# What holds back a gather: other F tiles for the holds, an earlier place for one block's gathers, and two scalings moved in the last unit

## The chip, the core and the metric

The kernel runs on one core of a Trainium2 chip. Its engines work from queues of their own and wait for each other through semaphores: PE (TensorE, matrix products; PEld is its weight loads), DVE (VectorE), ACT (ScalarE), POOL (GpSimd), and SP, whose queue issues the large loads. The metric is the device time of one execution in microseconds. Three runs of the kernel before took 372.48, 372.81 and 375.04 us; the median is 372.81.

## The reference, cut to what matters

A recurrent attention block is followed by a mixture of eight experts, of which each token uses one. All is float32.

```python
# attention, per batch b and head h, over t: state is 48x48
y[:, :, t] = einsum('bhd,bhde->bhe', rt, state + u*kt*vt)
state      = w * state + einsum('bhd,bhe->bhde', kt, vt)
# experts, per token x[b, s] of 384 numbers
e = argmax(logits) if s == 0 or local_gate < 0.5 else prev_e     # top expert or the previous token's
p = softmax(logits)
h = maximum(x[b, s] @ w1[e], 0.0)                                # 384 -> 1024
out[b, s] = p[e] * (h @ w2[e])                                   # 1024 -> 384
```

There are 4 x 768 tokens. A token's expert is known only when its attention output and the router's choice are there; its row is then gathered from memory, and its result scattered back.

## The kernel before, in words

The first part, up to about 105 us, is attention, and is not touched. The rest is the class Experts. It works through ten units, each one expert and a number of token slots. Units 0 and 1 are **plain** units of 168 slots (`HEAD`), worked while the router still sorts the second half of the tokens. Units 2 to 9 are the **blocks** of `BLOCKS = (448, 424, 392, 376, 336, 336, 256, 192)`, the experts in falling order of their token counts. Units 2 to 7 are **wide** (336 slots or more); unit 8 has a form of its own; unit 9, the last, is plain again. Unit 2 is the first large block, unit 3 the second, unit 4 the third with 392 slots: three gathers of 128 rows and a fourth of 8.

A unit's tokens come by `gather` (L1157): one indirect DMA from POOL's queue for each 128 rows, from `x_d` into a tile `xg`. PE turns `xg` (transposes, L1170) and ACT copies the result to `exT`. Then come the hidden layer (L1184 in plain units, L1265 in wide ones), the relu, and the second product (L1281, L1322, L1332, L1425). ACT scales a result by its gate (L1410, L1460), and POOL scatters it (L1415).

The hidden layer's result lies in eight **F tiles**, `u[0]` to `u[7]`, four in each tile `hg`. In a plain unit the relu (L1187) writes u[m] as soon as PE has done step m. In a wide unit a step of `twenty(i, g, ...)` makes tiles 4g to 4g + 3 by a scheme with fewer products: in ten steps s = 0 to 9, PE adds into two banks, ACT copies them out to `snap` (L1268), DVE joins these pieces in `hg` (L1252), and ACT does the relu (L1257 and L1260) **in place** on the same columns. The relus are put off by `self.owed`: u[4g + 2] gets its relu in step 5; u[4g] and u[4g + 1] only in step 0 of the half that follows, so u[4] and u[5] of a unit get theirs in step 0 of the next unit.

All engines' orders are written out by hand: the order of the calls in the code is the order of each queue. A gather would go out as soon as POOL reaches it. To hold it back, `gather` may have a tile `after`; POOL then first copies one column of that tile to a small tile `seen` (L1153), and so waits until it is written. `gathered(i, j, after)` does this for the gather j of unit i. The copy reads the tile as it stands at that place in the order; a write that comes later in the order has to wait until the copy has read.

Two other things lie near the change. In unit 1, at m = 4, POOL writes one element of unit 2's `w2t` from the last rows gathered for unit 2 (L1506), and SP loads that `w2t` only behind this. And `xg` has six buffers, so a gather also waits until the rows that were in its buffer have been turned. `weight_sums` (L1222, DVE) and `factors` (L1300, DVE) are sums of weights that the schemes need; `sums` (L1291, DVE) are those of F tiles.

In unit 9, at m = 2, the products of unit 8 are finished; `joined` makes DVE's seven steps (L1392), and `ends` holds the two scalings (ACT, L1410), each with its scatter.

Of the kernel before, what the change touches and what calls it, by code (L numbers as in the profile page):

```python
# [27 lines left out]
DK, FK = D // P, F // P  # L28
# [9 lines left out]
EARLY = 2  # L38
# [1029 lines left out]
class Experts:  # L1068
# [447 lines left out]
    def run(self, att, flag, ready, free):  # L1516
# [39 lines left out]
        def gathered(i, j, after):  # L1556
            if i < n and j < len(self.units[i]["rows"]):
                self.gather(i, slice(j, j + 1), after)
# [5 lines left out]
        def wide(i, g, s):  # L1564
            nonlocal behind
            u, r = self.units[i], self.router
            following = self.units[i + 1]["wide"]
            k, z = (i, 0) if g else (i - 1, 1)
            early = k < EARLY
            if s == 0:  # L1570
                behind = {} if early else self.seven(k, z)
                if early:
                    behind = {("1b", "3a")[m - FK + 2]: lambda m=m: self.output(k, m) for m in range(FK - 2, FK)}
            if s in (1, 2) and not early:
                self.sums(k, 2 * z + s - 1)
            at = (g * 10 + s - (5 if i == EARLY else 1))
            if (i, g, s) == (EARLY, 0, 2):
                self.routing(2 * FK)
            if (i, g) == (EARLY + 1, 0):
                for when, step in ((1, r.exceeded), (2, lambda: self.flag(0)), (3, lambda: r.halves(0)), (5, lambda: r.halves(E - 1)),  # L1580
                                 (6, lambda: self.flag(1, self.bank("fp"))), (8, lambda: self.flag(2))):
                    if s == when:
                        step()
            if at >= 0 and at % 2 == 0 and at < 8:
                turned(i + 1, at // 2)
            elif (g, s) in ((0, 9), (1, 1), (1, 3), (1, 5), (1, 7), (1, 9)) and (i, g) > (EARLY, 0):
                sent()
            fill(*BEHIND[s])
            if g == 0:
                if s == 0 and not early:  # L1590
                    fs.extend(self.factors(k, 3))
                if s == (8 if i == EARLY else 3):
                    fs.extend(self.factors(i, 0))
                some(fs, (0, 0, 0, 0, 0, 0, 0, 0, 2, 2)[s] if i == EARLY else (2, 1, 1, 3, 1, 0, 0, 0, 0, 0)[s])
                if s == 5 and following:
                    ws.extend(self.weight_sums(i + 1))
                some(ws, (0, 0, 0, 0, 0, 0, 0, 2, 2, 2)[s] if i == EARLY else (0, 0, 0, 0, 0, 3, 4, 3, 3, 0)[s])
                if i == EARLY and s == 4:
                    drained(k)
                    self.fetch(i + 1, self.nc.sync, 2)  # L1600
                if s == 9 and not early:
                    joined(k)
                    some(js, 3)
                if s == 8:
                    gathered(i + 2, 0, u[2])
            else:
                if s == 0:
                    gathered(i + 2, 1, u[0])
                    some(js, 9)
                some(ends, (0, 0, 1, 1, 0, 0, 0, 0, 0, 0)[s])  # L1610
                if s == 2:
                    fs.extend(self.factors(i, 1))
                    if following:
                        ts.extend(self.token_sums(i + 1))
                if s == 7:
                    fs.extend(self.factors(i, 2))
                some(ws, (3, 2, 1, 0, 0, 0, 4, 0, 0, 0)[s] if i == EARLY else (0, 2, 1, 0, 0, 0, 0, 0, 0, 0)[s])
                some(fs, (0, 0, 1, 3, 0, 0, 0, 1, 2, 1)[s])
                some(ts, (0, 0, 0, 0, 2, 4, 4, 2, 0, 0)[s])
                if s == 5:  # L1620
                    gathered(i + 2, 2, u[6])
                if s == 9:
                    gathered(i + 2, 3, u[4])

        for i in range(n):
            u = self.units[i]
            after = len(self.units[i + 1]["rows"]) if i + 1 < n else 0
            following = i + 1 < n and self.units[i + 1]["wide"]
            if u["wide"]:
                if i == EARLY:  # L1630
                    free()
                    self.snap = self.spare.tile([P, 6, 2, BLOCKS[0] // 2], F32, name="snap", tag="xT")
                self.fetch(i + 1, self.nc.sync, 1)
                for g in range(2):
                    self.twenty(i, g, lambda s: wide(i, g, s))
                continue

            if u["seven"]:

                order = [k for ks in BEHIND for k in ks if k != "hr"]  # L1640
                parts = (0, 1, 4, 8, 12, 15, 18)
                for m in range(FK):
                    if m == 0:
                        self.fetch(i + 1, self.nc.sync, 1)
                        behind = self.seven(i - 1, 1)
                        fs.extend(self.factors(i - 1, 3))
                    self.hidden(i, m)
                    self.settle()
                    if m < 2:
                        self.sums(i - 1, 2 + m)  # L1650
                    some(fs, 4)
                    fill(*order[parts[min(m, 6)]:parts[min(m + 1, 6)]])
                    if m in (2, 3):
                        fs.extend(self.factors(i, m - 2))
                    if m == 5:
                        joined(i - 1)
                        some(js, 9)
                    if m > 5:
                        some(ends, 1)
                    if m in (3, 4):  # L1660
                        turned(i + 1, m - 3)
                    else:
                        sent()
                continue

            lag = 4 if i == n - 1 else 1
            for m in range(FK):
                if following and m == FK - 1:
                    turned(i + 1, after - 1)
                self.hidden(i, m)  # L1670
                if (i, m) == (0, 0):
                    att.turn(B * HP - 1, yb[1:])
                if i == n - 1:
                    if m == 0:
                        behind = {**self.seven(i - 1, 0)}
                        for j in range(2):
                            self.sums(i - 1, j)
                        fill(*order)
                        for j in range(2, 4):
                            some(self.factors(i - 1, j), 4)  # L1680
                            self.sums(i - 1, j)
                    if m == 1:
                        behind = self.seven(i - 1, 1)
                        fill(*[k for k in order if k[1] == "a"])
                    if m == 2:
                        fill(*order)
                        joined(i - 1)
                        some(js, 9)
                        some(ends, 2)
                if sends and m >= 1 and i > EARLY:  # L1690
                    self.send(*sends.pop(0))
                if i == n - 1:
                    if m >= lag:
                        self.rows(m - lag)
                elif m >= lag and not (following and m > FK - 3):
                    self.output(i, m - lag)
                if i <= EARLY:
                    self.routing(i * FK + m)
                if i == 0 and m == 1:
                    self.fetch(1, self.nc.scalar)  # L1700
                if m >= FK - after and not (following and m == FK - 1):
                    (turned if following else self.turn)(i + 1, m - (FK - after))
                if following and m == 3:
                    ws.extend(self.weight_sums(i + 1))
                if following and m >= 3:
                    some(ws, 4)
            if i + 1 == EARLY:
                for j in range(len(self.units[i + 2]["rows"])):
                    gathered(i + 2, j, u[FK - 2 + j // 2])

            if following:
                self.output(i, FK - 3)
                some(self.token_sums(i + 1), 12)
                self.both = False
            elif i < n - 1:
                for m in range(FK - lag, FK):
                    self.output(i, m)
                drained(i)
# [198 lines left out]
```

## Time and profile before

| What | us |
|---|---|
| median of three runs | 372.81 |
| the profiled execution, as timed | 373.39 |
| its span in the trace | 371.7 |
| PE busy | 356.4 |
| DVE busy | 268.9 |
| POOL busy | 171.1 |
| ACT busy | 152.3 |

The granted TensorE clock was 0.993 of full speed over the span. PE is busy nearly throughout. In a time line, a row gives the start, the busy time, the engine, the line, the operation with its output and inputs, and in brackets the idle time ahead of it with what ended that. In a list of waits, a row gives who waited for whom, then the sum, the number of times and the longest.

### The profile page before, as it was taken

The page shows a single profiled execution, that of the slowest core. Times are in us where ns is not written, and L with a number is a line of the kernel's source. Part 1 is how long each engine was busy: PE and PEld are TensorE (multiplying, and loading weights), DVE is VectorE, ACT ScalarE, POOL GpSimd, SP SyncE. Part 2 cuts the span into 40 slices and gives each one's busy share as a digit, 9 for nine tenths or more (in the row PEclk, how much of TensorE's full clock was granted, in tenths as well). Part 3 has the DMA queues.
Part 4 walks back from the last instruction along what each step waited for, and adds up shares of the span by engine and source line. Part 5 has one row for each costly group of instructions (what it writes and reads, how often), then busy time and mean ns, then how long its engine had stood idle before and what let it go on. Part 6 is the DMA issues. An engine that isn't in the chain of part 4 may idle for free. (4 is left out here: it accounts for less than half of the span.)

```text
span 371.7 us, 9208 instructions
## 1 busy us (share of the span) xinstructions
PE 356.4 (96%) x3542; PEld 309.4 (83%) x3542; DVE 268.9 (72%) x766; ACT 152.3 (41%) x375; POOL 171.1 (46%) x212
## 2 busy tenths in 40 slices
PE   7999999899999999899799999999999999999992
PEld 4777877677679999788689999998998998889971
DVE  6887778788834877597689869879989957446400
ACT  4222232223523224654446546556555545423110
POOL 8879999689522056148274214403604114002022
PEclk9999999999999999999999999999999999999997
DMA  7999999982668656814116506426236426505011
GB/s 270 410 409 407 408 401 359 379 285 96 203 212 288 261 204 266 337 46 173 53 48 240 186 11 229 140 94 227 91 143 232 136 82 233 182 21 213 2 44 38
DMA packets 17380, 74.91 MB, mean 202 GB/s; under 512 B 2394, under 2 KB 6240, under 8 KB 15024
## 3 DMA queue, kind: packets, MB, share of 16 engines
q1 hardware_dynamic: 10336, 56.89, 41.0%
q0 software_dynamic: 3424, 9.48, 7.5%
q10 hardware_dynamic: 3568, 7.87, 5.7%
q8 instruction: 30, 0.49, 0.5%
q14 instruction: 22, 0.18, 0.1%
HBM read 64.79 MB, written 9.47 MB: 200 GB/s over the span
## 5 line engine op out<-in xcount | busy, mean ns | idle before, releaser
L1268 ACT COPY snap<-h 128x336 f32<-128x336 f32 (+4 forms) x120 | 57.6, 480 | 77.3 <-PE h L1265 74.6
L1415 POOL DMA_INDIRECT out_dram<-yo,sid x27 | 33.4, 1238 | 92.8 <-ACT yo L1410 77.1
L1157 POOL DMA_INDIRECT xg<-x_d,gid x29 | 31.6, 1090 | 28.6 <-DVE gid L924 19.3
L1153 POOL COPY seen<-hg 128x1 f32<-128x1 f32 x26 | 16.5, 633 | 54.3 <-ACT hg L1257 49.5
L1252 DVE TENSOR_TENSOR hg<-snap 128x336 f32<-128x336 f32 (+4 forms) x48 | 26.6, 554 | 19.5 <-ACT snap L1268 19.3
L1265 PE MATMUL h<-xs,ws 128*128 128x168 f32 (+4 forms) x192 | 39.4, 327 | 0.0
L1322 PE MATMUL y<-factors,sums 128*128 128x192 f32 x168 | 38.4, 327 | 0.0
L1184 PE MATMUL h<-exT,w1t 128*128 128x168 f32 (+2 forms) x192 | 37.1, 332 | 0.0
L324 DVE TENSOR_TENSOR am<-pair,kept 128x768 f32<-128x768 f32 x32 | 29.9, 951 | 9.9 <-PE pair L314 5.9
L1265 PEld LDWEIGHTS h<-xs,ws 128*128 128x128 f32 x192 | 32.5, 190 | 4.6 <-issue 1.2
L238 POOL TENSOR_TENSOR pd<-rk 128x384 f32<-128x384 f32 x32 | 31.8, 1015 | 7.6 <-PE y L295 5.6
L1184 PEld LDWEIGHTS h<-exT,w1t 128*128 128x128 f32 x192 | 31.0, 190 | 2.7 <-issue 0.5
L1322 PEld LDWEIGHTS y<-factors,sums 128*128 128x128 f32 x168 | 28.5, 190 | 0.1
L1332 PE MATMUL tp<-w2t,hg 128*80 128x384 f32 (+2 forms) x64 | 24.7, 488 | 1.9 <-ACT hg L1257 1.9
L1187 ACT ACTIVATE hg<-h 128x168 f32<-128x168 f32 (+2 forms) x32 | 10.6, 333 | 38.0 <-PE h L1184 37.1
L1322 PE MATMUL y<-w2t,hg 128*128 128x192 f32 x112 | 25.0, 328 | 0.0
L255 POOL TENSOR_TENSOR rw<-rk,tab 128x384 f32<-128x384 f32 x26 | 23.6, 929 | 0.9 <-DMA rk<-in_rk_dram 0.9
L352 ACT COPY xT<-y 128x768 f32<-128x768 f32 x15 | 12.0, 800 | 28.2 <-PE y L344 28.2
L331 PE MATMUL y<-am,kv 128*64 128x128 f32 x360 | 22.9, 277 | 0.3 <-DVE y L301 0.3
L234 POOL TENSOR_TENSOR ke<-kv,endT 128x288 f32<-128x288 f32 (+1 forms) x32 | 21.9, 705 | 1.5 <-DMA kv<-in_kv_dram 1.5
L1300 DVE TENSOR_TENSOR factors<-w2t 128x192 f32<-128x192 f32 x56 | 19.7, 351 | 2.9 <-PE y L1322 2.9
L1222 DVE TENSOR_TENSOR ws<-w1t 128x256 f32<-128x256 f32 x48 | 18.8, 418 | 3.6 <-DMA w1t<-in_w_dram 3.6
(293 smaller groups left out, 785.1 us busy)
## 6 DMA issues: line engine op xcount, KB each, us to landing
w1t<-in_w_dram SPq DMA_DIRECT2D x8, 1536.0 KB, 6.8
w2t<-in_w_dram SPq DMA_DIRECT2D x8, 1536.0 KB, 7.1
rk<-in_rk_dram SPq DMA_DIRECT2D x15, 768.0 KB, 9.8
kv<-in_kv_dram SPq DMA_DIRECT2D x16, 584.0 KB, 8.7
vT<-in_vT_dram SPq DMA_DIRECT2D x16, 384.0 KB, 7.4
x_d<-x ACTq DMA_DIRECT2D x4, 1152.0 KB, 9.3
w1t<-in_w_dram SPq DMA_DIRECT2D x2, 768.0 KB, 5.2
w2t<-in_w_dram SPq DMA_DIRECT2D x2, 768.0 KB, 4.7
```

Source lines behind the costliest of these rows:

```text
L238: nc.gpsimd.tensor_mul(t["pd"][:, z], t["rT"][:, z], t["kT"][:, z])
L255: engine.tensor_mul(t["rw"][:, z], t["rT"][:, z], spread(pw, 1, z.stop - z.start))
L324: return lambda: nc.vector.tensor_mul(t["am"][:, g], sc, spread(kept, 1, 2))
L331: nc.tensor.matmul(t["y"][h][p * DP:(p + 1) * DP, c2 * P:(c2 + 1) * P], lhsT=t["v"][:, (2 * c + h) * DH:(2 * c + h) * DH + DP], rhs=t["am" ...
L1157: self.nc.gpsimd.indirect_dma_start(out=xg[:n], out_offset=None, in_=self.x_d[:rows], in_offset=bass.IndirectOffsetOnAxis(ap=u["gid"][:n, ...
L1184: nc.tensor.matmul(h[:, :n], lhsT=u["w1"][:, m, kk, :], rhs=u["xT"][:, kk, :], start=(kk == 0), stop=(kk == DK - 1))
L1252: return lambda: nc.vector.tensor_tensor(o, a, self.snap[:, b, :, :n], op=Alu.add if op == "+" else Alu.subtract)
L1265: nc.tensor.matmul(bank[:, z * n:(z + 1) * n], lhsT=left(a), rhs=right(b), start=(k == 0 and z == 0), stop=(k == len(CHAINS[c]) - 1), skip ...
L1268: nc.scalar.copy(self.snap[:, place, :, :n], source[:, ::-1] if (c, k) in TURNED else source)
L1322: nc.tensor.matmul(bank[:, x * half:(x + 1) * half], lhsT=a(), rhs=b(), start=first, stop=(count(k) == FK // 2), skip_group_check=True)
L1332: nc.tensor.matmul(u["y"][:z, :D], lhsT=u[m][:, 2 * P:2 * P + z], rhs=h[:, m], start=first, stop=last)
L1415: self.nc.gpsimd.indirect_dma_start(out=out.rearrange("n (h d) -> (n h) d", h=2) if half else out, out_offset=bass.IndirectOffsetOnAxis(ap ...
```

## The change

Three edits, all in the hand-written order of the units.

1. In a wide unit i, in step 9 of the second half, the hold of unit i + 2's fourth gather reads u[6] in place of u[4]. Only unit 4 has a fourth gather at this place (unit 2 gets its gathers from the routing, unit 3 from unit 1, and later blocks have three or fewer).
2. The four gathers of unit 3 are given out in unit 1's steps m = 4, 5, 6, 7, held by u[3], u[4], u[5], u[6]. Before, they were given out after the last step, held by u[6], u[6], u[7], u[7].
3. In the last unit, the two scalings of unit 8, each with its scatter, are given out one at m = 3 and one at m = 4. Before, both were at m = 2.

```diff
                 if s == 9:
-                    gathered(i + 2, 3, u[4])
+                    gathered(i + 2, 3, u[6])
...
                         joined(i - 1)
                         some(js, 9)
-                        some(ends, 2)
+                    if m in (3, 4):
+                        some(ends, 1)
...
                 if following and m >= 3:
                     some(ws, 4)
-            if i + 1 == EARLY:
-                for j in range(len(self.units[i + 2]["rows"])):
-                    gathered(i + 2, j, u[FK - 2 + j // 2])
-
+                if following and m >= 4:
+                    gathered(i + 2, m - 4, u[m - 1])
```

The first place is POOL's queue at the end of unit 1. Here are its rows before: `hg_2115` is unit 1's tile of u[4] to u[7], `xg_2121` unit 2's last gather, `xg_2188` to `xg_2203` are unit 3's four; behind each row stands which queues' semaphores it waits for.

```order
L1506 COPY w2t_1990<-xg_2121 1x1 [waits DMAHW0_49,DMAHW1_49,DMASW7_49,PE_49]
L1153 COPY seen_125<-hg_2115 128x1 [waits Activation_49,Pool_49]
L1157 DMA xg_2188<-x_d_60,gid_79 128x384 [waits DMASW2_49]
L1153 COPY seen_125<-hg_2115 128x1 [waits Pool_49]
L1157 DMA xg_2193<-x_d_60,gid_79 128x384 [waits DMASW3_49]
L1153 COPY seen_125<-hg_2115 128x1 [waits Activation_49,Pool_49]
L1157 DMA xg_2198<-x_d_60,gid_79 128x384 [waits DMASW4_49,PE_49]
```

And the rows now, where `hg_2033` is unit 1's tile of u[0] to u[3]:

```order
L1506 COPY w2t_1990<-xg_2121 1x1 [waits DMAHW0_49,DMAHW1_49,DMASW7_49,PE_49]
L1153 COPY seen_125<-hg_2033 128x1 [waits Pool_49]
L1157 DMA xg_2150<-x_d_60,gid_79 128x384 [waits DMASW2_49]
L1153 COPY seen_125<-hg_2115 128x1 [waits Pool_49]
L1157 DMA xg_2171<-x_d_60,gid_79 128x384 [waits DMASW3_49]
L1153 COPY seen_125<-hg_2115 128x1 [waits Activation_49,Pool_49]
L1157 DMA xg_2189<-x_d_60,gid_79 128x384 [waits DMASW4_49,PE_49]
```

The operations stand in the same order on POOL, behind L1506 in both; the first hold has no wait for ACT left.

The second place is ACT's queue where unit 2 goes over into unit 3. `hg_2327` is unit 2's tile of u[4] to u[7], and L1257 is the relu of u[4], then of u[5]. Before:

```order
L1460 ACTIVATE yo_2482<-tp0_1789,gate0_97 40x384 [waits PE_49]
L1268 COPY snap_2228<-h_2235 128x2x212 [waits PE_49,Activation_49]
L1257 ACTIVATE hg_2327<-hg_2327 128x448 [waits DVE_49,Pool_49]
L1257 ACTIVATE hg_2327<-hg_2327 128x448
L1268 COPY snap_2228<-h_2236 128x2x212 [waits DVE_49,PE_49]
L1260 ACTIVATE hg_2327<-hg_2327 128x224 x2
```

Now:

```order
L1460 ACTIVATE yo_2482<-tp0_1789,gate0_97 40x384 [waits PE_49]
L1268 COPY snap_2228<-h_2235 128x2x212 [waits PE_49,Activation_49]
L1257 ACTIVATE hg_2327<-hg_2327 128x448 [waits DVE_49]
L1257 ACTIVATE hg_2327<-hg_2327 128x448
L1268 COPY snap_2228<-h_2236 128x2x212 [waits DVE_49,PE_49]
L1260 ACTIVATE hg_2327<-hg_2327 128x224 x2
```

No row has moved; the relu of u[4] no longer waits for POOL.

The third place is ACT's queue in the last unit, with - for before and + for now. L1187 is a relu, L1389 the first step of joining unit 8's products, L1410 a scaling.

```order
 L1187 ACTIVATE hg<-h 128x192 x3
 L1389 COPY t<-y_3962 128x192
-L1410 ACTIVATE yo<-yo,gate 128x384 x2
-L1187 ACTIVATE hg<-h 128x192 x5
+L1187 ACTIVATE hg<-h 128x192
+L1410 ACTIVATE yo<-yo,gate 128x384
+L1187 ACTIVATE hg<-h 128x192
+L1410 ACTIVATE yo<-yo,gate 128x384
+L1187 ACTIVATE hg<-h 128x192 x3
```

The relus of m = 3 and m = 4 now stand ahead of the first and the second scaling. The scatters keep their order on POOL, and PE, DVE and SP keep theirs throughout.

## The prediction, made before the changed kernel ran

> **What bounds the kernel now.** I read the page's head first, then what PE waits for, then what ACT waits for, then the time lines of the four engines around the one wait that stands out.
>
> ```profile
> span 371.7 us, 9208 instructions
> PE 356.4 (96%) x3542; PEld 309.4 (83%) x3542; DVE 268.9 (72%) x766; ACT 152.3 (41%) x375; POOL 171.1 (46%) x212
> ...
> PE tp L1332 <- ACT hg L1257: 1.9, 1, 1.9
> ...
> PE tp L1170 <- DMA xg<-x_d,gid: 0.7, 1, 0.7
> PE tp L1170 <- ACT snap L1268: 0.6, 1, 0.6
> ...
> ACT hg L1257 <- POOL seen L1153: 2.7, 1, 2.7
> ```
>
> PE works through 96% of the span, so only a wait of PE, or a lengthening of its tail, can show in the time. Its largest single wait is 1.9 us: L1332 waits for an F tile's relu (L1257). The last line says what that relu waited for: a POOL copy into `seen`, L1153, the copy by which gathers are held back. The two 0.6 and 0.7 us waits of L1170 (a block's rows turned) also lie where the change works. Here are the engines around the large wait, PE first, then ACT, then DVE.
>
> ```profile
> 176.50 0.49 PE L1322 MATMUL y<-w2t,hg 128*128 128x192 f32 x2
> 178.90 1.56 PE L1332 MATMUL tp<-w2t,hg 128*128 128x384 f32 x4 [1.91 <-ACT hg L1257]
> ...
> 175.07 0.51 ACT L1268 COPY snap<-h 128x424 f32<-128x424 f32 x1
> 178.27 1.04 ACT L1257 ACTIVATE hg<-hg 128x448 f32<-128x448 f32 x2 [2.69 <-POOL seen L1153]
> ...
> 175.46 0.36 DVE L1300 TENSOR_TENSOR factors<-w2t,factors 128x192 f32<-128x192 f32 x1
> 179.35 0.29 DVE L1291 TENSOR_TENSOR sums<-hg 128x128 f32<-128x128 f32 x1 [3.53 <-ACT hg L1257]
> ```
>
> And POOL:
>
> ```profile
> 167.82 6.23 POOL L1415 DMA_INDIRECT out_dram<-yo,sid  x1 [2.94 <-ACT yo L1460]
> 174.01 0.24 POOL L1153 COPY seen<-hg 128x1 f32<-128x1 f32 x1
> 174.40 1.06 POOL L1157 DMA_INDIRECT xg<-x_d,gid  x1 [0.16 <-PE tp L1458]
> 175.77 1.02 POOL L1415 DMA_INDIRECT out_dram<-yo,sid  x1 [0.31 <-ACT snap L1268]
> 177.09 0.94 POOL L1415 DMA_INDIRECT out_dram<-yo,sid  x1 [0.30 <-issue]
> 178.03 0.21 POOL L1153 COPY seen<-hg 128x1 f32<-128x1 f32 x1
> 178.43 0.99 POOL L1157 DMA_INDIRECT xg<-x_d,gid  x1 [0.19 <-issue]
> 189.11 4.78 POOL L1153 COPY seen<-hg 128x1 f32<-128x1 f32 x1
> ```
>
> The copy at 178.03 is the hold of unit 4's fourth gather. It starts with no idle time before it, so it waits for nothing: POOL has only got there late, behind a scatter that spans 6.23 us. It reads u[4] before that tile's relu, which works in place, so the relu may not write until the copy has read. ACT stands 2.69 us, PE 1.91, DVE 3.53.
>
> **Part 1, u[4] becomes u[6].** The order rows show both halves of the effect: POOL's copy stays in its place, and ACT's relu of u[4] loses its wait for POOL. ACT is then free when its snap ends, 175.07 + 0.51 = 175.58; the two relus take 1.04 and end at 176.62, the first at about 176.1. PE ends its earlier work at 176.50 + 0.49 = 176.99, so the first relu is there 0.9 us ahead. The second serves the second half of L1332, over 0.7 us later. PE gains all of its wait, **1.91 us**; that is the upper end for this part, and nothing in it costs PE time.
>
> What is late next? DVE restarts behind the relus, at 176.66 in place of 179.35, 2.69 us earlier, while PE gains 1.91: DVE moves ahead of PE by 0.78. After 178.90 the trace shows no wait of PE until its last matmul, so the gain should run through to the end. The weights' fetches wait for PE's use of the buffers and move with it.
>
> POOL loses a quiet stretch. Its scatter at 177.09 and copy at 178.03 ran while DVE stood; now DVE runs from 176.66. That such copies can be held is seen in the copy at 189.11, which spans 4.78 us, to 193.89, until DVE pauses:
>
> ```profile
> 193.27 0.58 DVE L1252 TENSOR_TENSOR hg<-snap 128x424 f32<-128x424 f32 x1
> 194.97 0.36 DVE L1392 TENSOR_TENSOR yo<-y,t 128x192 f32<-128x192 f32 x1 [1.12 <-ACT t L1389]
> ...
> xg<-x_d,gid POOLq DMA_INDIRECT x1, 2.3
> ...
> 189.24 0.35 PE L1170 MATMUL tp<-ident,xg 8*128 8x8 f32 x3
> ```
>
> The gather behind it (8 rows, 2.3 us from issue to landing) is asked for by PE at 189.24, after the change at 187.33, so it must start by 185.03. Unheld it starts at 178.43; with one hold of 4.78 on its copy at 178.03 + 4.78 + 0.16 = 182.97. Both are in time: cost zero. Only two holds in a row are not, a rival below.
>
> The Trainium skill, page "SBUF — State Buffer", section "Who interferes with whom", says that a DVE instruction with two SBUF inputs contends with a GpSimd instruction that reads SBUF, and holds the shared ports for its own length. By that rule a copy is held for one DVE instruction, under 0.8 us, the gather starts by about 179.3 the sum is the same, and the slower rival's chance would go to the forecast. The 4.78 us span a whole run of such instructions, so the trace goes further than the rule here, and I keep the rival.
>
> **Part 2, the second large block's gathers.** Instructions and their order on POOL stay; what changes is what the four holds wait for.
>
> ```profile
> 140.11 1.03 POOL L1506 COPY w2t<-xg 1x1 f32<-1x1 f32 x1 [1.85 <-PE tp L1170]
> 141.41 0.18 POOL L1153 COPY seen<-hg 128x1 f32<-128x1 f32 x1 [0.26 <-ACT hg L1187]
> 142.18 1.15 POOL L1157 DMA_INDIRECT xg<-x_d,gid  x1 [0.59 <-issue]
> ...
> xg<-x_d,gid POOLq DMA_INDIRECT x1, 8.4
> ...
> 150.67 0.52 PE L1170 MATMUL tp<-ident,xg 128*128 128x128 f32 x3 [0.72 <-DMA xg<-x_d,gid]
> 153.33 0.52 PE L1170 MATMUL tp<-ident,xg 128*128 128x128 f32 x3 [0.63 <-ACT snap L1268]
> ```
>
> In the code one expects gathers up to four matmul groups earlier; POOL does not allow it. The copy L1506, which waits for unit 2's last gather, stands ahead of all four in both kernels and ends at 141.14. Only the first hold then waits, 0.26 us, and the gap behind it may shrink from 0.59 to the 0.16 seen behind holds that did not wait. So the gathers start 0.26 to 0.69 us earlier. The first lands 8.4 us after its issue (the row of transfers above), at 150.58, just when PE resumes at 150.67. PE's 0.72 us could shrink by that shift, or not at all if the transfers stand behind the weights anyway.
>
> But the gain meets the next wait on the way:
>
> ```profile
> 154.52 0.76 DVE L1222 TENSOR_TENSOR ws<-w1t 128x256 f32<-128x256 f32 x2 [1.29 <-DMA w1t<-in_w_dram]
> 158.81 0.61 DVE L1252 TENSOR_TENSOR hg<-snap 128x448 f32<-128x448 f32 x1
> 159.51 0.53 ACT L1268 COPY snap<-h 128x448 f32<-128x448 f32 x1 [0.76 <-DVE hg L1252]
> ...
> 158.55 1.45 PE L1332 MATMUL tp<-w2t,hg 128*128 128x384 f32 x4
> 160.10 1.02 PE L1265 MATMUL h<-exT,ws 128*128 128x224 f32 x4
> ```
>
> DVE resumes at 154.52 when the next unit's w1 lands, then runs without a pause; its join of 158.81 releases ACT's snap, which ends at 160.04, and PE goes on at 160.10, having ended at 160.00. An earlier PE would stand at 160.10 for the same weights. So part 2 is worth **0**: at most −0.10 us while w1 lands when it does. Without that bound it could be the 0.72 + 0.63 = 1.35 of both waits, of which a shift of 0.69 takes 0.69. On the other side gathers that move ahead of w1 delay it: up to +0.3 us, my estimate from half the shift.
>
> **Part 3, the two scalings of the last unit.**
>
> ```profile
> 352.35 1.14 ACT L1410 ACTIVATE yo<-yo,gate 128x384 f32<-128x384 f32 x2 [2.03 <-DVE yo L1392]
> 353.40 0.53 ACT L1187 ACTIVATE hg<-h 128x192 f32<-128x192 f32 x2
> ...
> 351.37 2.11 PE L1184 MATMUL h<-exT,w1t 128*128 128x192 f32 x12
> 353.32 0.81 PE L1425 MATMUL y<-w2t,hg 128*128 128x384 f32 x2
> ...
> 362.50 0.97 POOL L1415 DMA_INDIRECT out_dram<-yo,sid  x1 [7.02 <-DVE yo L1442]
> ```
>
> The scalings delay the relus of m = 3 and 4 to 353.40, but PE goes from L1184 to L1425 with no gap and the trace shows it none later. After the change the first relu comes about 0.9 us earlier; nobody waits for it. The two scatters go out up to about half a us later, near 355; POOL has then 7 us of rest before the last ones at 362.5. Value 0; the bounds are the ACT work itself, ±0.5 us, if the matmuls' modelled ends hide a stall or the scalings now delay m = 4.
>
> **The sum.** The profiled execution took 373.39 us, 1.69 beyond its span: 373.39 − 1.91 ± 0 = 371.5. It stands 0.58 above the median of 372.81; I take the same difference from the median: 372.81 − 1.91 = **370.9**. Its own range is −0.7 (part 2 unbounded by w1) to +0.8 (parts 2 and 3 cost): 370.2 to 371.7.
>
> **The rivals.**
>
> Given back, or not there: the wait grew out of one late scatter; in a plain execution POOL may be earlier, or something follows PE closely enough to take the 1.91 back. For it: DVE is busy almost without a gap from 179.35 to 193.85. Against: DVE moves forward more than PE. Time 372.8.
>
> Part 2 pays too: w1 lands earlier because the gathers are out of its way, and both waits of L1170 go. 370.9 − 1.35 = 369.6. Against: the bytes ahead of w1 stay the same.
>
> Slower: the gather behind the moved POOL work is held twice in DVE's now longer run. Scatter held 6.23 (the row at 167.82): 177.09 + 6.23 = 183.32; copy held 4.78: about 188.1; gather at 188.3, landed at 190.6. PE, at 187.33, would stand 3.2 us and the net is −1.91 + 3.2 = +1.3: 374.1. It decides from a gather start of 185.03. Against it: it takes two of the longest spans in a row.
>
> That the change doesn't do what it says holds for part 2 already, since POOL's order keeps the gathers where they were; it is in the forecast.
>
> **How the numbers follow.** Forecast 0.70, given back 0.15, part 2 pays too 0.08, slower 0.07. The range 369.9 to 372.9 takes the forecast's own range and the given-back case, with some of the earlier one; the slower case and the full 1.35 stay out. A measurement of this kernel tells about 1% (3.7 us) from no change. No case comes to that by itself: 369.6 is 0.9% faster, 374.1 is 0.3% slower. So within 1% has 0.93; 0.04 for faster (369.6 and 0.4 us that I don't see), 0.03 for slower.
>
> **What would show it.** In the changed kernel's profile: no wait of ACT's L1257 for POOL's `seen`, none of PE's L1332 for L1257; L1332 at about 177.0 with DVE's sums at 176.7, if the time before is unchanged; L1170's waits near 150 and 153 smaller, and a new wait of about that size near 160; unit 4's 8-row turn near 187.3 unheld; the last L1432 matmuls 1.9 us earlier. The prediction is wrong if PE shows a new wait between 177 and 362, or if the stretch before 160 moves by more than 0.3 us.

## The result: 0.5% less, and the wait is gone

In 20 runs each, the kernel before has a median of 373.15 us and the changed kernel 371.49 us. The ratio is 0.9949, with a 95% interval of 0.9927 to 0.9971. By the ratio that is 1.9 us less, with 1.1 to 2.7 us as its interval; the medians differ by 1.66. The profiled execution of the changed kernel took 370.74 us, with a span of 369.0. A ratio here and below is not the quotient of the two medians printed beside it; among other things it leaves out the few runs that were over 1.5% above the fastest of their kernel, which the medians keep.

Here is what PE waited for in the changed kernel, the whole list that the view gives:

```profile
PE pair L177 <- POOL ident masks.py:199: 1.6, 1, 1.6
PE tp L1170 <- DMA xg<-x_d,gid: 0.8, 3, 0.3
PE pair L194 <- ACT step L203: 0.6, 1, 0.6
PE mp L277 <- POOL ke L234: 0.3, 1, 0.3
PE pair L321 <- issue: 0.3, 1, 0.3
```

The wait of L1332 for the relu L1257 doesn't stand in it any more; no wait of the list lies behind 155 us. Here is the same place in the changed kernel's time lines, PE, ACT, DVE and POOL:

```profile
176.03 0.49 PE L1322 MATMUL y<-w2t,hg 128*128 128x192 f32 x2
176.36 1.45 PE L1332 MATMUL tp<-w2t,hg 128*128 128x384 f32 x4
...
174.59 0.51 ACT L1268 COPY snap<-h 128x424 f32<-128x424 f32 x1
175.00 1.05 ACT L1257 ACTIVATE hg<-hg 128x448 f32<-128x448 f32 x2
...
176.08 0.29 DVE L1291 TENSOR_TENSOR sums<-hg 128x128 f32<-128x128 f32 x1 [0.74 <-ACT hg L1257]
...
167.35 6.22 POOL L1415 DMA_INDIRECT out_dram<-yo,sid  x1 [2.93 <-ACT yo L1460]
177.55 0.25 POOL L1153 COPY seen<-hg 128x1 f32<-128x1 f32 x1
177.98 0.99 POOL L1157 DMA_INDIRECT xg<-x_d,gid  x1 [0.19 <-issue]
```

POOL is as late as it was: its scatter spans 6.22 us and its copy comes at 177.55. But the relus run right behind ACT's snap, 2.5 us ahead of that copy.

The spans differ by 2.7 us, more than the medians. Where it comes from is read at places that all kernels share. The table has the starts of four: a product of unit 1 (L1281), the L1265 that follows the wait for w1, the L1332 of the large wait, and the last products (L1432).

| us | L1281 | L1265 | L1332 | L1432 |
|---|---|---|---|---|
| before | 144.84 | 160.10 | 178.90 | 361.50 |
| after | 144.39 | 159.63 | 176.36 | 358.84 |
| difference | -0.45 | -0.47 | -2.54 | -2.66 |

0.45 us are there already before the first changed instruction (POOL's L1506, ahead of it, starts at 140.11 and 139.66), in work that the change doesn't touch. The first large step, from L1281 to L1265, takes 15.26 us before and 15.24 after: the earlier gathers bring nothing. Then 2.07 us go at L1332 and 0.12 just behind it; from there to the end nothing more is won or lost.

### The profile page after: what moved, and what is told of

Read it like the earlier page. It is cut to its first block, busy times and chain, and to the rows that moved or that the text cites. A ratio compares the mean times of both kernels' runs of the same rounds, so it can differ in the third digit from the quotient of the medians.

```text
span 369.0 us, 9210 instructions
## 1 busy us (share of the span) xinstructions
PE 357.6 (97%) x3542; PEld 309.7 (84%) x3542; DVE 269.5 (73%) x766; ACT 152.3 (41%) x375; POOL 170.5 (46%) x212
## 5 line engine op out<-in xcount | busy, mean ns | idle before, releaser
L1265 PE MATMUL h<-xs,ws 128*128 128x168 f32 (+4 forms) x192 | 39.4, 328 | 0.0
L1265 PEld LDWEIGHTS h<-xs,ws 128*128 128x128 f32 x192 | 32.5, 190 | 4.6 <-issue 1.2
L1187 ACT ACTIVATE hg<-h 128x168 f32<-128x168 f32 (+2 forms) x32 | 10.7, 334 | 40.0 <-PE h L1184 38.9
L1332 PE MATMUL tp<-w2t,hg 128*80 128x384 f32 (+2 forms) x64 | 24.7, 488 | 0.1
```

The costliest lines, as they stand in the source:

```text
L1265: nc.tensor.matmul(bank[:, z * n:(z + 1) * n], lhsT=left(a), rhs=right(b), start=(k == 0 and z == 0), stop=(k == len(CHAINS[c]) - 1), skip ...
L1332: nc.tensor.matmul(u["y"][:z, :D], lhsT=u[m][:, 2 * P:2 * P + z], rhs=h[:, m], start=first, stop=last)
```

## The experiments

All times are compared with the kernel before on the same chip (median 373.87 us for the first four, 373.88 for the others).

**Each edit alone.** The first has only the other tile for the fourth gather's hold:

```diff
-                    gathered(i + 2, 3, u[4])
+                    gathered(i + 2, 3, u[6])
```

> Only the hold of unit 4's fourth gather is changed, from u[4] to u[6]. Theory: the whole gain is PE's wait for the relu of u[4], which had to wait for POOL's copy. The wait goes (1.9 us by the trace before, 2.1 to 2.2 counted from PE's usual spacing of its products), so the ratio to the kernel before is about 0.995, the same as for all three edits. Rival, the gathers or the scalings carry a part of it: under half the gain, 0.997 or more.

Measured: 371.16 us, ratio 0.9961 (0.993 to 0.9992). In its trace L1332 starts 31.84 us behind L1281 (176.55 and 144.71), against 34.06 before and 31.97 after. PE's waits at the gathers, and DVE's at w1, are nearly those of before, as its time lines show:

```profile
150.35 0.52 PE L1170 MATMUL tp<-ident,xg 128*128 128x128 f32 x3 [0.54 <-DMA xg<-x_d,gid]
153.02 0.52 PE L1170 MATMUL tp<-ident,xg 128*128 128x128 f32 x3 [0.64 <-issue]
154.24 0.76 DVE L1222 TENSOR_TENSOR ws<-w1t 128x256 f32<-128x256 f32 x2 [1.33 <-DMA w1t<-in_w_dram]
159.82 1.02 PE L1265 MATMUL h<-exT,ws 128*128 128x224 f32 x4
```

So by the trace this one word carries the change; the time agrees, with an interval too wide to show it alone. The second kernel has only unit 3's gathers in unit 1's steps 4 to 7:

```diff
-            if i + 1 == EARLY:
-                for j in range(len(self.units[i + 2]["rows"])):
-                    gathered(i + 2, j, u[FK - 2 + j // 2])
...
+                if following and m >= 4:
+                    gathered(i + 2, m - 4, u[m - 1])
```

> Only the earlier place of unit 3's gathers. Theory: they start about 0.75 us earlier and PE's two waits near 150 and 153 us shrink from 1.35 to about 0.7 in sum, but PE stands again before 160 us, because DVE's joins are late behind the weight sums that wait for w1. L1265 near 160.1 doesn't move against the start of the Experts, and the ratio is 1.000 within 0.1%. Rival, the gain runs on: L1265 earlier by 0.4 to 0.7 us, ratio 0.998 to 0.999.

Measured: 375.19 us, ratio 1.0018 (0.9981 to 1.0055). PE's wait sum at the three turns near 150, 153 and 155 us falls, but L1265 stands 5.58 us behind DVE's wait for w1, as in the kernel before (time lines of PE and DVE):

```profile
152.87 0.52 PE L1170 MATMUL tp<-ident,xg 128*128 128x128 f32 x3 [0.38 <-DMA xg<-x_d,gid]
154.91 0.76 DVE L1222 TENSOR_TENSOR ws<-w1t 128x256 f32<-128x256 f32 x2 [1.90 <-DMA w1t<-in_w_dram]
160.49 1.02 PE L1265 MATMUL h<-exT,ws 128*128 128x224 f32 x4
```

From L1281 (145.06) to L1265 it takes 15.43 us, 0.17 more than before. DVE waits longer, 1.90 in place of 1.29: what PE gains, it brings to DVE, which can't use it.

The third has only the scalings later:

```diff
-                        some(ends, 2)
+                    if m in (3, 4):
+                        some(ends, 1)
```

> Only the two scalings of the last unit later. Theory: the relus of m = 3 and 4 come up to 0.9 us earlier and the two scatters up to 0.6 us later, PE's products keep their places and the last scatter too: ratio 1.000. Rival, PE's matmuls hide a stall that ends earlier: up to 0.5 us, 0.9987.

Measured: 373.26 us, ratio 0.9996 (0.9964 to 1.0027). In the time line of the changed kernel, which has this edit too, ACT's and PE's rows read:

```profile
349.89 0.33 ACT L1187 ACTIVATE hg<-h 128x192 f32<-128x192 f32 x1 [2.23 <-PE h L1184]
350.12 0.61 ACT L1410 ACTIVATE yo<-yo,gate 128x384 f32<-128x384 f32 x1
350.87 0.33 ACT L1187 ACTIVATE hg<-h 128x192 f32<-128x192 f32 x1
351.09 0.61 ACT L1410 ACTIVATE yo<-yo,gate 128x384 f32<-128x384 f32 x1
...
350.67 0.81 PE L1425 MATMUL y<-w2t,hg 128*128 128x384 f32 x2
```

L1425 stands 1.96 us behind the start of the two products ahead of it (348.71), as before (353.32 and 351.37, 1.95). In the trace of the kernel with this edit alone it is 1.95 us too (352.55 and 354.50). The relus moved, and nothing was waiting for them.

**Is it the relu or POOL's queue?** The changed kernel, with the hold on the other late tile:

```diff
-                    gathered(i + 2, 3, u[6])
+                    gathered(i + 2, 3, u[5])
```

> The changed kernel, but the fourth gather's hold reads u[5], whose relu is as late as that of u[4] and is the second of the two. Theory: what costs is the relu that may not write before POOL's copy has read. The relu of u[4] now runs without a wait, that of u[5] waits for the copy (to about 177.8 us on the changed kernel's clock), and PE stands about 1.3 us between the second and third product of L1332: the time lies 1.3 us above the changed kernel, ratio to before about 0.9985. Rival, the wait came from POOL's late queue whatever the tile (the gathers behind it): no wait of PE, 0.995 as in the changed kernel.

Measured: 372.55 us, ratio 0.9975 (0.994 to 1.0009), 1.4 us above the kernel with only u[6] by the medians. The two intervals overlap, so the trace has to decide. In its lists of waits, PE's and ACT's, the pair is back:

```profile
PE tp L1332 <- ACT hg L1257: 1.3, 1, 1.3
...
ACT hg L1257 <- POOL seen L1153: 2.2, 1, 2.2
```

And in PE's time line:

```profile
176.47 0.81 PE L1332 MATMUL tp<-w2t,hg 128*128 128x384 f32 x2
178.55 0.91 PE L1332 MATMUL tp<-w2t,hg 128*128 128x384 f32 x2 [1.26 <-ACT hg L1257]
```

L1332 now falls apart at the tile that is held: its first two products run, the two that read u[5] wait. POOL's rows are the same as in the changed kernel. The wait belongs to the relu that has to let the copy read first, and the theory holds.

**Why POOL is late.** The kernel before, with the hold on u[4] as it was, and four tiny DVE instructions without an SBUF input put into DVE's run:

```diff
+                if i == EARLY and s in (3, 4, 5, 6):
+                    self.nc.vector.memset(self.pause, 0.0)
                 if s == 5:
                     gathered(i + 2, 2, u[6])
```

> The kernel before (hold on u[4], nothing else changed) with four DVE memsets of one column (no input from SBUF) in steps 3 to 6 of unit 2's second half, inside DVE's unbroken run of sums of two SBUF tiles. Theory: POOL's scatter near 167.8 us spans 6.2 us because its reads find no opening in that run. With openings it spans under 2 us, POOL reaches the copy of u[4] 4 us or so earlier, the relu isn't held and most of PE's 2 us wait goes, ratio 0.995. Rival, the scatter is long for another reason (its queue, its transfers): it still spans about 6 us, the wait stays, ratio 1.000 or 0.1% above for the memsets.

Measured: 371.71 us, ratio 0.9948 (0.9925 to 0.9972). In its time lines (lines are numbered one higher in this kernel):

```profile
167.82 1.17 POOL L1416 DMA_INDIRECT out_dram<-yo,sid  x1 [2.94 <-ACT yo L1461]
...
174.40 0.58 ACT L1461 ACTIVATE yo<-tp,gate 40x384 f32<-40x384 f32 x1
175.28 0.96 POOL L1416 DMA_INDIRECT out_dram<-yo,sid  x1 [3.28 <-DVE hg L1253]
176.24 0.21 POOL L1154 COPY seen<-hg 128x1 f32<-128x1 f32 x1
...
176.48 1.04 ACT L1258 ACTIVATE hg<-hg 128x448 f32<-128x448 f32 x2 [0.90 <-POOL seen L1154]
...
177.11 1.56 PE L1333 MATMUL tp<-w2t,hg 128*128 128x384 f32 x4
```

The scatter falls from 6.23 to 1.17 us; in the nine other kernels it spans 5.77 to 6.37. The copy comes only 1.8 us earlier, not 4, because the last scatter ahead of it then has to wait for its own scaled rows, which are there at 174.98 (the bracket names a join of DVE that ended later). That is enough to take ACT's wait from 2.69 to 0.90 and to bring PE's L1333 from 178.90 to 177.11. So what DVE does is what makes POOL late: four memsets alone take the hold away, and by the times they are a cure as good as the edit.

How they do it is not shown. The expectation was an opening in DVE's run, but here are DVE's rows around the scatter:

```profile
167.41 0.42 DVE L1223 TENSOR_TENSOR ws<-ws 128x256 f32<-128x256 f32 x1
167.43 0.06 DVE L1622 MEMSET pause<- 128x1 f32 x1
167.74 0.41 DVE L1223 TENSOR_TENSOR ws<-ws 128x256 f32<-128x256 f32 x1
168.08 0.75 DVE L1223 TENSOR_TENSOR ws<-w1t 128x256 f32<-128x256 f32 x2
168.75 0.37 DVE L1209 TENSOR_TENSOR more<-exT,xs 128x212 f32<-128x212 f32 x1
...
169.95 0.06 DVE L1622 MEMSET pause<- 128x1 f32 x1
```

No memset lies within the scatter's span, 167.82 to 168.99. The nearest ends 0.33 us ahead of it. DVE's sums run through the span without a gap, and POOL gets its work done all the same. Either that memset changes something which lasts, or it matters that DVE's run is 0.04 us later against the scatter (its sum starts at 167.41, before at 167.37). Against the second speaks the kernel with later sums, further below, where the scatter starts at yet another place between two sums and is held for 5.77 us. No run tells the two apart.

The page "SBUF — State Buffer" of the Trainium skill, section "Who interferes with whom", says that such instructions contend with GpSimd's reads. The trace agrees: in the kernel before, the copy of 4.78 us ends at 193.89 and DVE's run at 193.85. But this hold lasts over a run of many of them and not for one. The section infers that descriptor generation isn't touched by them; here the scatter is held for 5 us, though the trace doesn't say in which part of its work.

**Why the gathers bring nothing.** Three variants of the changed kernel. The first takes two of DVE's weight sums, those that meet the wait for w1, out of unit 2's first half and gives them out in the second:

```diff
-                some(ws, (0, 0, 0, 0, 0, 0, 0, 2, 2, 2)[s] if i == EARLY ...
+                some(ws, (0, 0, 0, 0, 0, 0, 0, 0, 2, 2)[s] if i == EARLY ...
...
-                some(ws, (3, 2, 1, 0, 0, 0, 4, 0, 0, 0)[s] if i == EARLY ...
+                some(ws, (3, 2, 3, 0, 0, 0, 4, 0, 0, 0)[s] if i == EARLY ...
```

> The changed kernel with the first two weight sums of unit 3 (DVE, those that wait for w1) given out 11 steps later, in step 2 of unit 2's second half. Theory: these sums at the head of DVE's queue are what takes back the gathers' gain before 160 us. DVE's joins no longer wait for w1 there, PE keeps the 0.4 us that it is ahead at 157 us in the changed kernel, and the time falls by 0.3 to 0.5 us more, ratio to before about 0.994. Rival, the gain is lost for another reason (ACT's relus, PE's own order): L1265 near 159.6 us doesn't move and the ratio stays 0.995.

Measured: 370.18 us, ratio 0.9931 (0.9893 to 0.9969). DVE still reaches a sum that needs w1 at 154.25, but its joins are ahead of it now, and L1265 comes 4.91 us behind it in place of 5.58 (time lines of DVE and PE):

```profile
154.25 0.76 DVE L1222 TENSOR_TENSOR ws<-w1t 128x256 f32<-128x256 f32 x2 [0.49 <-DMA w1t<-in_w_dram]
157.14 0.38 PE L1170 MATMUL tp<-ident,xg 40*128 40x40 f32 x3
159.16 0.92 PE L1265 MATMUL h<-exT,ws 128*128 128x224 f32 x4
```

From L1281 (144.47) it is 14.69 us, 0.55 less than in the changed kernel; 0.3 to 0.5 was expected.

The second puts unit 3's first gather ahead of the copy L1506, into POOL's idle stretch:

```diff
+            self.gather(EARLY + 1, slice(0, 1), self.units[1][3])
             u = self.units[EARLY]
             self.nc.gpsimd.tensor_copy(u["w2"][0:1, 0, 0:1], u["xg"][-1][0:1, 0:1])
...
-                if following and m >= 4:
+                if following and m > 4:
                     gathered(i + 2, m - 4, u[m - 1])
```

> The changed kernel with the first of unit 3's gathers ahead of the copy L1506, in POOL's idle stretch of 1.85 us. Theory: the gather then lands before the weights' load begins, about 8 us earlier than before, and the others start 1.4 us earlier; the waits of L1170 near 150 and 152 us go, but the weight sums behind w1 still set PE's place at 160 us: ratio 0.995 as in the changed kernel. Rival, the place near 160 us follows the gathers: 0.7 us less, 0.993.

Measured: 370.53 us, ratio 0.9911 (0.9881 to 0.994). Here the theory missed a part. PE's waits for gathers are gone as expected, but L1265 (161.97) is only 14.66 us behind L1281 (147.31), 0.58 less than in the changed kernel. Still it is 5.58 us behind DVE's wait for w1, as DVE's and PE's time lines show:

```profile
156.39 0.76 DVE L1222 TENSOR_TENSOR ws<-w1t 128x256 f32<-128x256 f32 x2 [1.47 <-DMA w1t<-in_w_dram]
158.52 0.38 PE L1170 MATMUL tp<-ident,xg 40*128 40x40 f32 x3
160.31 1.53 PE L1332 MATMUL tp<-w2t,hg 128*128 128x384 f32 x4 [0.88 <-ACT hg L1257]
161.97 1.02 PE L1265 MATMUL h<-exT,ws 128*128 128x224 f32 x4
```

The row of w1's load among the transfers, with its KB and the us from issue to landing:

```profile
w1t<-in_w_dram SPq DMA_DIRECT2D x1, 1536.0 KB, 11.2
```

So w1 still sets the place; but w1 itself landed 11.2 us after its issue, where in the changed kernel it took 11.8. From its issue to DVE's start behind it, it took 11.70 to 12.03 us in the eight kernels whose gathers all stand behind L1506, and 11.25 here, so this is more than their spread. My reading is that a gather which has landed before the weights' load begins takes no more of the transfers' time from it. That is the prediction's rival "part 2 pays too", which the change itself does not reach, as its gathers stay behind L1506.

The third has both of these edits.

> Both: the first gather ahead of L1506 and the first two weight sums later. Theory: neither the gathers nor w1 holds PE between 148 and 160 us, PE's waits there (about 1.0 us in sum in the changed kernel) go and stay gone: 0.8 to 1.0 us under the changed kernel, ratio to before about 0.9925. Rival: the sum of the two single effects is lost later to DVE, which is busy nearly throughout the second half of unit 2: 0.995.

Measured: 368.85 us, ratio 0.9884 (0.9851 to 0.9917). This is the fastest kernel of the study, 1.2% under the kernel before. In its time lines neither DVE at w1 nor PE waits at this place (a row with a wait has it in brackets):

```profile
152.82 0.75 DVE L1222 TENSOR_TENSOR ws<-w1t 128x256 f32<-128x256 f32 x2
155.12 0.38 PE L1170 MATMUL tp<-ident,xg 40*128 40x40 f32 x3
157.14 0.92 PE L1265 MATMUL h<-exT,ws 128*128 128x224 f32 x4
```

From L1281 (143.91) to L1265 it takes 13.23 us, 2.01 less than in the changed kernel, where 0.8 to 1.0 was expected. The two single gains are 0.55 and 0.58; together they give 0.9 us more than their sum. The traces show where this comes from, if the stretch is cut at PE's turn of the last 40 rows of unit 3 (L1170). Before and in the changed kernel that turn reads:

```profile
157.82 0.38 PE L1170 MATMUL tp<-ident,xg 40*128 40x40 f32 x3
...
156.94 0.38 PE L1170 MATMUL tp<-ident,xg 40*128 40x40 f32 x3
```

| us | L1281 to the turn | the turn to L1265 |
|---|---|---|
| before | 12.98 | 2.28 |
| after | 12.55 | 2.69 |
| later sums | 12.67 | 2.02 |
| first gather ahead | 11.21 | 3.45 |
| both | 11.21 | 2.02 |

Against the kernel with both edits, the gathers cost the changed kernel 1.34 us in the first part, and the wait for w1 0.67 us in the second. Later sums alone remove only the second. The gather ahead alone removes the first, and 0.76 of its 1.34 us is taken back in the second, where PE arrives earlier and waits longer. Both edits leave neither.

## Why the prediction was right

**The large wait.** Right in kind and place: the copy into `seen` read u[4] late, the relu had to let it, PE stood. It is shown by three kernels: the edit alone takes the wait away, the hold on u[5] brings it back at the other tile, and an earlier POOL shortens it. The size of 1.91 us was a little low. PE started L1332 0.33 us behind the product ahead of it once nothing was in the way (176.03 and 176.36), so that the wait before was 178.90 − 176.50 − 0.33 = 2.07 us; the trace's 1.91 counts from the modelled end of that product. With the 0.12 us of a slower restart behind it the trace gains 2.2 us. The measured 1.1 to 2.7 us can't tell the two sizes apart.

**What is late next: nothing.** DVE restarts 16.45 us behind L1265 (176.08 and 159.63) in place of 19.25, 2.80 earlier where the step had 2.69. The gain of L1332 stands at L1432. The rival "given back" fell.

**POOL's loss of a quiet stretch.** No loss: the copy at 177.55 spans 0.25 us and the 8-row gather starts at 177.98, 6 us ahead of where it would have cost (PE turns its rows at 186.59, and it lands 2.4 us after its issue). The "slower" rival did not happen; what it needs, a scatter held 6 us, exists, but not at this place.

**The gathers.** Right: 0, though by a hair outside one bound. The first started 1.30 us behind L1506's start (140.96 and 139.66) in place of 2.07, which is 0.77 us earlier where 0.26 to 0.69 was given. As forecast, the gain meets the next wait: up to the turn of 40 rows PE is 0.43 us ahead (12.55 in place of 12.98), and 0.41 of it is gone at L1265. The new wait that was expected near 160 is in no list, because it falls apart into 0.30 us at L1332, which waits for a relu behind DVE's join, and 0.11 at L1265. PE's two waits of 0.72 and 0.63 became 0.34 and 0.33 with a shorter third. PE's L1265 stands 5.58 us behind DVE's wait for w1 in five kernels, those of the three single edits, before and after, whatever the gathers do; taking the sums away from there breaks this. The 0.3 us that the prediction allowed for gathers that delay w1 did not come: w1's load took 11.84 us, before 11.85. With a gather wholly out of the way it comes 0.6 us earlier. The prediction called itself wrong if the stretch before 160 moved by more than 0.3 us. L1265 did move by 0.47, but 0.45 of it is the shift from ahead of the change, and 0.02 is left.

**The scalings.** Right: 0.

**The sum.** 372.81 − 1.91 = 370.9 was forecast, 371.49 measured. The median of before in the longer series is 373.15; the difference, 1.66 by the medians and 1.9 by the ratio, is that of the forecast. Of the 0.6 us between the two times, 0.34 comes from the median that the forecast started from.

## What to carry to other kernels

A hold that only reads a tile to delay something is also a reader, and a later write in place has to wait for it; take for it a tile that nobody writes any more. When a wait for data is shortened, look for the next wait on the same engine's way that depends on neither, here a load at the head of another engine's queue: what is gained ahead of it is given back there, here 0.41 of 0.43 us and 0.76 of 1.34. An order that holds a slow queue behind a marker (POOL's copy L1506) can make an edit in the code mean less than it reads.

## What the runs showed that was not expected

A wait of PE of about 2 us can cost more than itself. In the profiles of the gathers alone and of the scalings alone, which keep the large wait, PE runs at a granted clock of 0.50 for some 3.4 us soon behind it; in the profile of the kernel before, with the same wait, it doesn't. Here are stretches of 2 us of the kernel with only the gathers; the columns are the busy time of PE, PEld, DVE, ACT and POOL, the granted clock, and the transfers' share and rate:

```profile
178.00:180.00 2.00, 0.70 (x2) 0.48 (x3) 0.26 (x1) 1.33 (x3) 1.62 (x3) 1.00 0.31 117
180.00:182.00 2.00, 2.00 (x7) 1.55 (x6) 1.83 (x11) 1.04 (x4) 0.00 (x0) 0.65 0.03 6
182.00:184.00 2.00, 2.00 (x8) 1.97 (x7) 1.88 (x13) 0.51 (x1) 0.00 (x0) 0.50 0.00 0
184.00:186.00 2.00, 2.00 (x15) 1.96 (x14) 1.86 (x9) 0.89 (x2) 0.00 (x0) 1.00 0.00 0
```

From L1332 to the L1265 of step 3 it takes 6.14 us (179.30 to 185.44) in place of 4.46 before (178.90 to 183.36): 1.7 us on top of the wait. The variant with the first gather ahead shows the same behind a wait of 2.00 us in the attention part, near 95 us, where the granted clock is 0.50. Behind the 1.26 us of the hold on u[5] it doesn't show. The Trainium skill, page "TensorE: Matmul & The Clock Gate", Part 1, gives an idle window of about 3.4 us before the clock is halved, and a warm-up of the same length; the length of the slow stretch agrees, but here waits of 1.9 and 2.0 us were enough, in three of four profiles that have one. No profile shows such a drop without one, until PE's work is done. So the edit also takes away a risk of 1.7 us in part of the executions. It can't be frequent: the trace gains 2.2 us without it and the measured gain is at most 2.7, which leaves it 0.5 us on average at most, an estimate.
